# Windowed attention and a gated MLP on one core: two blocks' values with V stationary and sums by ones, first queries scaled in their cast, a negated maximum, and a new order

## The chip, the cores and the metric

The kernel runs on one core of one Trainium2 chip. The metric is device time in microseconds of one execution, as the median over runs; a profile is of one execution. Engines in the tables: PE is TensorE (PEld its weight loads), DVE is VectorE, ACT is ScalarE, POOL is GpSimd, SP is SyncE, which here only issues transfers.

## The reference, cut to what matters

Attention for 4 batches of 8 heads, 768 positions and 64 dimensions a head, in which each position sees the 4 first keys ("sinks") and a window of the 128 last ones; then the heads side by side (512 columns) through two matrices with a quick GELU between.

```python
scores = scale * np.matmul(q, k.transpose(0, 1, 3, 2))        # scale = 1/8
keep = is_sink | in_window                                    # 4 sinks, window 128
scores = np.where(keep, scores, -1000000000.0)
a = np.exp(scores - np.max(scores, axis=-1, keepdims=True))
a = a / (np.sum(a, axis=-1, keepdims=True) + 1e-09)
attn_out = np.matmul(a, v)
x = attn_out.transpose(0, 2, 1, 3).reshape(3072, 512)
h = x @ w_in                                                  # 512 x 2048
g = h * (1.0 / (1.0 + np.exp(-1.702 * h)))
out = g @ w_out                                               # 2048 x 512
```

## The kernel before

**Blocks.** The 3072 positions are 24 blocks of 128; block b is part b % 6 of batch b // 6. They are worked in the order 0, 6, 12, 18 (the first block of each batch, which sees only itself), then 1 to 5, 7 to 11 and so on, which also see the block ahead of them and the sinks. Operations carry the block's number, and "_0" or "_1" for a half, that is four heads.

**A block's operations** and their names: q, k, v are loads with a cast to 16 bits on POOL's queue; tq and tk are its turns on PE (lines 379 to 399 for the first six blocks, of whose loads each partition holds eight neighbouring positions), cq and ck their copies or casts from PSUM into qkT; msk writes the mask of a first block into PSUM ahead of its scores (line 464); sc are the scores (478, 483); mx the row maximum (545); nb the maximum times -1/8 as the bias of the exponential (557), for first blocks alone; bx their exponentials, four instructions a half (568); in the other blocks pk puts the two blocks' scores in one place by a mask (535), sb subtracts the maximum (582) and ex is the exponential (606); ta are turns of the weights on PE (650) and ca their copies into "at"; for later blocks a transfer does that (tat), and sp and so on POOL select what belongs to the own block and to the one ahead (637). ks and vsb prepare the sinks' keys and values, snk are the sinks' scores and ms their maximum.

**Values.** av (line 703) multiplies the turned weights, as the stationary operand, with v65, that is V with a column of ones, 65 columns a head: PSUM gets 128 positions by 4 heads by 65, with the sum of the weights in the last column. nm takes the reciprocal of the four sums (722) and multiplies (723) into xn. tx turns xn back on PE (740), and cx copies it to xT, for the first eight blocks; later ones by a transfer (txd).

**MLP.** Blocks go in groups: [0], [6], [12, 18], then in twos. hG_u is a piece of the first product of group G (786: sixteen matmuls for a single block, four chunks of w_in at a time; wi0 to wi3 are w_in's quarters, and h0_u and h1_u use quarter u). The gate of the first three groups is a tanh on ACT (th, 800) and a product on DVE (g, 807); of the others one activation (816). oB_n is a quarter of the second product of block B (836, quarter n of w_out, loads wo0 to wo3); ev copies it from PSUM and st stores it. The last block's output goes in two pieces, of 320 columns (o23_0 to o23_3) and of 192 (o23_10 to o23_13).

**Buffers** are rings: "mm" in PSUM has three, "sc" two, "av" one. A buffer of "av" holds values or the sinks' scores from the PE step until nm or ms has read it; both kinds take turns in it.

**Order.** The operations are numbered as the program adds them, and ORDER lists all of them in one line of numbers, with a letter where an operation may run on several engines (d for DVE, a ACT, p POOL, s SP). Each engine works off its own in that order, in order. Waits follow from the data and the buffers.

```python
LD, LW, QKX, ATX, XTX, STX, SPX2 = 0.97, 2.55, 1.55, 1.56, 0.77, 0.85, 1.9
NB = {0: (0, 1), 6: (0, 1), 12: (0, 1), 18: (0, 1)}
RING = dict(qkn=4, qkn2=3, e32=3, a16=4, at=4, atp=3, ss=3, xn=3, xt=4, gt1=2, gt2=2, osb=4, mm=3, sc=2, av=1, th=2)
```

Of the kernel before, what the change touches and what calls it, by code (L numbers as in the profile page):

```python
# [54 lines left out]
ORDER = """
1a 9 6 8d 100 15 4a 5a 11 14 7 96 0a 23 94 21 3s 98 17 2s 29 18 104 107 105a 101p 102 103d 16 108 171 20 109 150 19
172a 10 95d 125 110 24 112 225 111 99d 26 151a 113 126d 27 114 115 97d 88 127 106 128a 130 92 226d 116a 117 12 90 129
148 118a 119 13 131 149a 22 120 194 132 121 86 196 195a 135 173 197a 87 133 122 134 89 123 199 124a 200 138 30 136 613
139d 137 25 152 142 174a 140 143 153 614 141d 615 154 91 144 155 619 156 145 157 158 146 616 93 620 147d 159 160 621
637 32 617 634 638 618 176 639 635 631 36 175 636 177 632 610 178 633 161 611 181 35 628 162a 179 612 180 163 182 165  # L60
622 164d 166 629 184 183 33 167 623 185d 168 39 198 630 169 31 204 640 170a 205 188 227 189 641 228a 201 28 230 186
206 642 231 209 202 624 187a 203 215 190 38 643 208 191 207 229 216d 210 644a 192 217 235 211 43 193a 625 232 212a 236
41 280 282 626a 256 281d 258 213 283a 627 233 652 259a 214 237 257a 649 653 218 238 234 261 661 241 40 650 262 654 239
285 37 260 651 662 242 286 304 44 655 266 243a 263 34 219 656 646 663 42 657 658 647 244 220 664 648 659 245 267 670
45 665 660 240 221 671 264 268 246 672 247a 269 265 248 667 222 270 249 666 250 284 668 271 251 48 676 669 46 290 252
323 673 47 253 287 677 291 254 306 272 678 288 255a 674a 223 292 679 273 224a 293 289 682 680d 294 51 307 305 683 50
688 295 308 311 49 686 309 675 52 684 687 312 689 692 310 685 313 276 693 690 314 277 296 315 704 297 344 324 345 705
327 691 316 53 330 325 694 326 361 331 274 695 696 275 328 698 697 681 332 278 317 699 279a 333 329 298 334 318 343
299 700 346 54 347 300 706 55 349 335 701 57 301 350 302 645 319 303a 707 348 702a 352 351 716 708a 320 353 362 336
321 717 354 720 322 337 365 724 709 59 721 363 399 714 364 368 60 712 715 703 369 725 722 366 713 340 355 723 710 341  # L70
367 718 711 356 371 370 338 719 732 64 339 372 726 342 56 733 62 382 381 373 61 383 727 387 384 359 734 360 385 728
388 401 735 390 386 729 374 419 389 750 402 391 375 730d 400 736d 751 748 392 67 406 403 742 66 404 752 65 743 407 749
740 63 753 378 738 379 408 376 739 744 377 393 409 357 405 745 746 358 741 394 420 380 747 439 58 410 754 440 423 421
760 422 426 397 755 427 411 398 761 424 457 756 425 762 428 757 429 430 412 766 758d 438 759 413 767 763 431 444 69
441 770 737 442 71 768 771 445 72 764a 772 769 446 68 416 443 773 780 432 447 417 788 781 433 448 414 774 415 73 458
459 789 775 460 449 464 395 778 396 461 776 418 779 465 782 777 462 436 495 450 783 463 466 790 75 765 437 731 784 467
74 468 434 451 785 435 476 791 482 786d 800 792a 479 454 793 801 798 469 455 794 514 452 795 802 453 808 803 456 477
804 809 478 470 799 483 796 480 471 806 797 485 805 484 816 76 481 810 77 486 474 80 496 475 817 70 502 807 499 487
497 82 811 498 78 500 818 503 81 516 822 504 819 823 505 517 501 812 820a 506 515 821 824 488 518 813 489 825 507 828
814d 83 472 826 552 473 79 519 832 827 521 829 535 836 833 536 522 492 837 834 508 523 830 524 493 509 520 844 831 84  # L80
835 490 534 525 491 845 540 494 541 838 537 846 526 542 839 538 512 787 847 513 543 840 539 544 553 852 848a 545 527
573 864 853 574 590 528 510 841 511 865 559 860 842d 529 546 861 556 862 530 850 547 554 854 851 555 85 560 531 855
856 532 557 858 533 857 561 866 859 558 550 815 562 591 563 551 872 597 867 863 592 564 873 593 598 868 843 594 548
849 880 595 869 596 881 600 565 888 599 549 874 889 870d 566 601 886 875 884 876a 602 567 885 572 568 878 877 575 569
879 892 570 578 882 571 893 603 576 887 890 579 604 894 891 577 883 900 580 581 895 582 901 607 912 608 583 896 913
605 871 897 606 902 898a 910 584 916 911 585 914 917 918 915 908 919 906 909 586 907 903 587 922 588 920 589 923 609
921 904a 928 924 929 925 930 926d 946 931 947 934 942 935 932a 948 943 933 940 905 927 936 941 899 938 937 949 944 939
956 945 950 957 951 958 952 962 953 963 954a 959 964 955 960d 965 961 966d 967
# [67 lines left out]
def kernel(  # L156
# [72 lines left out]
    z_s = plan.add("zs", DVE, 0.25, lambda: nc.vector.memset(vsa, 1.0), key=-897)  # L229
    z_a = [  # L230
# [133 lines left out]
    for pos, b in enumerate(BLOCKS):  # L364
# [5 lines left out]
        qkb = qkT[:, SLOT[b]]  # L370


        buf, n, unit = tunit[b]
        if b in OCT:
            parts = []
            before = used_slot.pop(SLOT[b], [])
            for w in (1, 0):
                tp = ps("mm", (P, 8, 4, 16), FP32, f"t{'qk'[w]}{b}")

                def t_qk(w=w, buf=buf, n=n, tp=tp):  # L380
                    for t in range(8):
                        for l in range(2):
                            nc.tensor.matmul(
                                tp()[64 * l : 64 * l + 64, t], buf()[:, n, w, t],
                                ident.rearrange("p (j l u) -> p l j u", l=2, u=16)[:, l], start=True, stop=True,
                            )
# [5 lines left out]
                parts.append(  # L392
                    plan.add(
                        f"c{'qk'[w]}{b}", {DVE: 0.6, ACT: 0.5}, 0,
                        lambda e, w=w, tp=tp, qkb=qkb: copy(
                            e, qkb[:, 4 * w : 4 * w + 4].rearrange("p c (u t) -> p c u t", t=8),
                            tp().rearrange("p t c u -> p c u t"),
                        ),
                        deps=[a] + before, give=[tp], key=K0 - 40,
                    )  # L400
                )
            o_qkt[b] = parts
        elif b in TQ:
# [37 lines left out]
        if r == 0:  # L441

            def sink_keys(bb=bb, qkb=qkb):
                for hl in range(2):
                    rows = slice(64 * hl, 64 * hl + 64)
                    nc.vector.tensor_copy(
# [3 lines left out]
            o_ks[bb] = plan.add(f"ks{b}", DVE, 0.45, sink_keys, deps=o_qkt[b] + [z_k], key=K0 - 10)  # L450
# [79 lines left out]
        for hf in range(2):  # L530
# [12 lines left out]
            def rowmax(hf=hf, t=sc[hf], own=own, small=small, ms=ms):  # L543
# [156 lines left out]
        for hf in range(2):  # L700
# [34 lines left out]
        if b in TX:  # L735
# [163 lines left out]
```

## Time and profile before

| what | value |
|---|---|
| median of 3 runs (lowest to highest) | 233.0 us (232.78 to 233.21) |
| the profiled execution's own time; its span | 232.43 us; 230.7 us |
| busy: PE, DVE, ACT, POOL | 217.0, 154.5, 139.8, 111.2 us |
| PE's granted clock | 1.00 throughout |
| costliest on PE: first product (L786), second (L836) | 93.2 us in 832, 92.1 us in 400 |
| costliest on DVE: maximum (L545) | 32.7 us in 48 |
| chain that ended last, by engine | PE 35%, ACT 2%, issue 1% |

How to read it: a line of the timeline gives start, time and what ran, with the idle time before it and what ended that in brackets; neighbours on PE overlap, since a matmul's time includes its way through the array, so the pace is read from start to start. A line of groups gives busy time and mean ns of one, then idle time before. A line of stretches gives for each engine its busy time, with the number of instructions in brackets, then PE's clock, the DMA share and GB/s. "DMA to landing" is the time from a transfer's issue to its arrival.

### The profile page before, as it was taken

The numbers are of one execution on the slowest core, as the hardware profiler recorded it, in microseconds if no ns is written. First come the engines' busy times: TensorE is split into PE (matmuls) and PEld (weight loads), VectorE is DVE, ScalarE is ACT, GpSimd is POOL, SyncE is SP. The second block draws the span as 40 slices with busy tenths as digits, with TensorE's granted clock in tenths as the row PEclk, the third lists the DMA queues.
The fourth block names the chain that finished last, engine by engine and source line by source line (L and its number), as shares of the span: only waits on it lengthen the run. The fifth ranks groups of instructions, "written<-read, shape, count | busy, mean of one in ns | idle before, by whom it ended". The sixth has DMA issues, their size and how long they took to land. (4 is left out here: it accounts for less than half of the span.)

```text
span 230.7 us, 5431 instructions
## 1 busy us (share of the span) xinstructions
PE 217.0 (94%) x2202; PEld 151.6 (66%) x2202; DVE 154.5 (67%) x388; ACT 139.8 (61%) x220; POOL 111.2 (48%) x129
## 2 busy tenths in 40 slices
PE   0878899999999999999999999999999999999994
PEld 0666865876586686486577496486686686775863
DVE  2487899999979976987797848668577847121001
ACT  2278774874597687168378386786358486631531
POOL 8983435995393869077392619265350312300000
PEclk9999999999999999999999999999999999999999
DMA  5999999999999899999999989999647542402312
GB/s 76 167 189 200 206 198 180 168 134 91 153 182 168 159 242 131 148 162 135 165 196 136 196 172 131 131 185 110 140 92 114 142 99 45 99 0 45 114 71 91
DMA packets 120904, 32.07 MB, mean 139 GB/s; under 512 B 112016, under 2 KB 117936, under 8 KB 120880
## 3 DMA queue, kind: packets, MB, share of 16 engines
q0 software_dynamic: 69888, 13.64, 72.2%
q1 hardware_dynamic: 50512, 17.96, 38.7%
q8 instruction: 17, 0.28, 0.5%
q10 hardware_dynamic: 480, 0.13, 0.3%
q14 instruction: 7, 0.06, 0.1%
HBM read 27.46 MB, written 6.29 MB: 146 GB/s over the span
## 5 line engine op out<-in xcount | busy, mean ns | idle before, releaser
L786 PE MATMUL hT<-xT,w_in 128*128 128x256 f16 (+1 forms) x832 | 93.2, 264 | 1.5 <-ACT gT L816 0.5
L836 PE MATMUL o<-w_out,gT 128*128 128x512 f16 (+2 forms) x400 | 92.1, 371 | 0.0
L786 PEld LDWEIGHTS <-w_in 128*128 128x128 f16 x832 | 73.9, 98 | 14.1 <-issue 3.7
L816 ACT ACTIVATE gT<-hT 128x512 f16<-128x512 f32 x80 | 45.8, 597 | 33.1 <-PE hT L786 32.9
L836 PEld LDWEIGHTS <-gT 128*128 128x128 f16 x400 | 36.1, 98 | 33.3 <-issue 1.9
L637 POOL TENSOR_SCALAR_AFFINE_SELECT atp<-at 128x1024 f16<-128x1024 f16 (+1 forms) x22 | 22.3, 1015 | 72.9 <-DMA at<-a 69.9
L545 DVE TENSOR_REDUCE mx<-sc 128x4 f32<-128x512 f32 x48 | 32.7, 683 | 0.8 <-PE sc L478 0.5
L606 ACT ACTIVATE a<-e 128x1056 f16<-128x1056 f32 (+2 forms) x24 | 22.5, 938 | 15.4 <-issue 12.5
L535 DVE COPY_PREDICATED sc<-later,sc 128x512 f32<-128x512 uint16 x40 | 26.8, 689 | 3.6 <-PE sc L483 3.3
L582 DVE TENSOR_TENSOR e<-sc,mx 128x512 f32<-128x512 f32 x40 | 26.7, 684 | 0.7
L722 DVE RECIPROCAL rcp<-av 128x4 f32<-128x4 f32 x48 | 8.6, 179 | 24.0 <-PE av L712 22.1
L637 POOL TENSOR_SCALAR_AFFINE_SELECT at<-at 128x1024 f16<-128x1024 f16 (+1 forms) x22 | 22.2, 1009 | 1.4
L271 POOL DMA_DIRECT2D v<-in_v_dram x24 | 21.7, 906 | 2.0 <-DMA w_in<-in_moe_w_in_dram 1.2
L723 DVE TENSOR_TENSOR xn<-av,rcp 128x256 f16<-128x256 f32 x48 | 20.4, 424 | 1.7
L241 DVE COPY osb<-o 128x512 f32<-128x512 f32 (+2 forms) x10 | 6.3, 634 | 21.2 <-PE o L836 21.1
L606 ACT ACT_TABLE_LOAD x12 | 15.4, 1283 | 6.1 <-DVE e L596 4.0
L318 POOL DMA_DIRECT2D qkn<-in_q_dram x18 | 16.1, 897 | 4.5 <-DMA w_out<-in_moe_w_out_dram 1.6
L816 ACT ACT_TABLE_LOAD x13 | 16.7, 1283 | 2.4 <-PE hT L786 1.8
L318 POOL DMA_DIRECT2D qkn<-in_k_dram x18 | 16.0, 890 | 3.6 <-DMA w_out<-in_moe_w_out_dram 3.4
L710 PE MATMUL av<-v,at 128*128 128x65 f16 x192 | 17.5, 195 | 0.1
L710 PEld LDWEIGHTS <-at 128*128 128x128 f16 x192 | 14.4, 98 | 2.7 <-DVE at L241 0.3
L712 PE MATMUL av<-v,atp 128*128 128x65 f16 x160 | 15.1, 194 | 0.0
(58 smaller groups left out, 198.1 us busy)
## 6 DMA issues: line engine op xcount, KB each, us to landing
out_dram<-osb SPq DMA_DIRECT2D x23, 256.0 KB, 3.2
qkn<-in_q_dram POOLq DMA_DIRECT2D x24, 128.0 KB, 5.7
qkn<-in_k_dram POOLq DMA_DIRECT2D x24, 128.0 KB, 5.4
v<-in_v_dram POOLq DMA_DIRECT2D x24, 128.0 KB, 5.5
w_in<-in_moe_w_in_dram POOLq DMA_DIRECT2D x4, 512.0 KB, 10.4
w_out<-in_moe_w_out_dram POOLq DMA_DIRECT2D x4, 512.0 KB, 15.4
at<-a SPq DMA_TRANSPOSE x18, 3.7
qkT<-qkn SPq DMA_TRANSPOSE x10, 4.3
```

Of the source, the lines that this page charges most:

```text
L271: f"v{b}", POOL, 0.88, lambda b=b, view=view: nc.gpsimd.dma_start(v65[:, b, :, 0:D], view),
L318: lambda buf=buf, n=n, w=w, view=view: nc.gpsimd.dma_start(buf()[:, n, "qk".index(w)], view),
L535: nc.vector.copy_predicated(out=t()[:, :, :, own].rearrange("p l j s -> p (l j) s"), mask=later.unsqueeze(1).to_broadcast((P, 4, P)), data ...
L545: nc.vector.tensor_reduce(out=part, in_=t()[:, :, :, own], axis=AX.X, op=ALU.max)
L582: nc.vector.tensor_tensor(out=e32()[:, 512 * hf : 512 * hf + 512].rearrange("p (l j s) -> p l j s", l=2, j=2), in0=t()[:, :, :, own], in1= ...
L606: nc.scalar.activation(out=a16()[:, lo:hi], in_=e32()[:, lo:hi], func=AF.Exp, scale=scale)
L637: nc.gpsimd.affine_select(out=dst, in_=at()[:, lo : lo + num], pattern=[[0, num], [1 if own else -1, P]], compare_op=ALU.is_ge if own else ...
L710: nc.tensor.matmul(av()[:, i], at()[:, c], v65[:, b, h], start=(r == 0), stop=(r == 0))
L723: nc.vector.tensor_tensor(out=xn()[:, xi, 4 * hf : 4 * hf + 4].rearrange("p (j l) d -> p l j d", l=2), in0=av()[:, :, 0:D].rearrange("p (l ...
L786: nc.tensor.matmul(ht()[:, n].rearrange("p (n t) -> p n t", n=NT), w_in16[:, c, bass.ts(f, P)], t0()[:, i0 : i0 + NT, c], start=(c == 0), ...
L816: lambda fs=fs, gt=gt, ht=ht: nc.scalar.activation(out=gt()[:, fs[0] : fs[-1] + 1], in_=ht(), func=AF.Gelu_apprx_sigmoid),
L836: nc.tensor.matmul(po()[:, 0:width], gt()[:, F, bass.ts(t, P)], w_out16[:, F, c0 : c0 + width], start=(F == 0), stop=(F == NF - 1),)
```

## The change

1. **Values of blocks 0 and 6** (AVT). V is stationary, 64 columns a head, and the turned weights stream. Two heads' outputs lie one under the other, on partitions 0 to 63 and 64 to 127, as 64 dimensions by 128 positions: already the form of xT. The sums come from a product of a 128 x 64 matrix of ones with the weights, so each of the 64 partitions holds the sum of its column. A half of a block takes two matmuls of 256 columns and four of 128 where it took four of 65. The normalization takes the reciprocal of 256 numbers a partition and multiplies 256, straight into xT. tx0, tx6, cx0 and cx6 go; one memset of the ones (zo) comes.
2. **First blocks' queries** (NEGATE, blocks 0, 6, 12, 18) get the factor 1/8 in their cast; the row maximum is written negated and is itself the bias; the eight nb go.
3. **The sinks' keys** may be copied on POOL too; here all stay on DVE. Some costs in the plan's table are other numbers; they have no effect on what is emitted.
4. **A new ORDER.**

```diff
+NEGATE = True
+AVT = {0,6}
 ...
+    ones = const.tile([P, D], FP16, name="ones")
+    z_o = plan.add("zo", DVE, 0.12, lambda: nc.vector.memset(ones, 1.0), key=-890)
 ...
+        prescaled = NEGATE and b in NB
+        qf = [scale if prescaled else 1.0, 1.0]
 ...
                         lambda e, w=w, tp=tp, qkb=qkb, qf=qf: copy(
                             e, qkb[:, 4 * w : 4 * w + 4].rearrange("p c (u t) -> p c u t", t=8),
-                            tp().rearrange("p t c u -> p c u t"),
+                            tp().rearrange("p t c u -> p c u t"), qf[w],
                         ),
 ...
+                if neg:
+                    nc.vector.tensor_reduce(out=part, in_=t()[:, :, :, own], axis=AX.X, op=ALU.max, negate=True)
+                    return
 ...
-                    nbias = const.tile([P, 8], FP32, name=f"nb{b}")
+                    nbias = small if prescaled else const.tile([P, 8], FP32, name=f"nb{b}")
 ...
-                o = plan.add(f"nb{b}_{hf}", DVE, 0.09, neg, deps=[o], key=K0 - 29)
-                def bexp(hf=hf, t=sc[hf], own=own, a16=a16, nbias=nbias):
+                if not prescaled:
+                    o = plan.add(f"nb{b}_{hf}", DVE, 0.09, neg, deps=[o], key=K0 - 29)
+                def bexp(hf=hf, t=sc[hf], own=own, a16=a16, nbias=nbias, scale=1.0 if prescaled else scale):
 ...
+        for hf in range(2 if b in AVT else 0):
+            av = ps(AVR.get((b, hf), "av"), (P, 2, 2, P), FP32, f"av{b}_{hf}")
+            rc = sb("e32", (P, 2, P), FP32, f"rc{b}_{hf}")
+            xt, ti = xts[b]
+            def turned(hf=hf, av=av, at=at, b=b):
+                for l in range(2):
+                    rows = slice(64 * l, 64 * l + 64)
+                    c = 4 * hf + 2 * l
+                    nc.tensor.matmul(av()[rows, 1], ones, at()[:, c : c + 2], start=True, stop=True)
+                for l in range(2):
+                    rows = slice(64 * l, 64 * l + 64)
+                    for jj in range(2):
+                        c = 4 * hf + 2 * l + jj
+                        nc.tensor.matmul(
+                            av()[rows, 0, jj], v65[:, b, head(c), 0:D], at()[:, c], start=True, stop=True
+                        )
 ...
+            def norm_t(hf=hf, av=av, rc=rc, xt=xt, ti=ti):
+                nc.vector.reciprocal(out=rc(), in_=av()[:, 1])
+                nc.vector.tensor_tensor(out=xt()[:, ti, 2 * hf : 2 * hf + 2], in0=av()[:, 0], in1=rc(), op=ALU.mult)
 ...
-        for hf in range(2):
+        for hf in range(0 if b in AVT else 2):
 ...
-        if b in TX:
+        if b in AVT:
+            pass
+        elif b in TX:
```

**The order's beginning**, by engine, with the numbers read back into names. Before:

```
PE   tq0 msk0 tk0 sc0 tk18 tq12 tk6 tk2 ta0_0 tq6 msk6 ta0_1 tk12 av0_0 sc6 tk1 av0_1 tq1 tq18 tx0 snk1 ta6_0
     h0_1 av6_0 ta6_1 msk12 sc12 av6_1 h0_3 tx6 h0_2 h1_3 h1_2 msk18 h1_1 sc18 h0_0 ta12_0 h1_0 ta12_1 av12_0
     o0_0 ta18_0 av12_1 o0_1 sc1 tx12 o6_0 av18_0 tq2 o6_1 snk2
DVE  zs zk zv za1 z1 ck0 mx0_0 za0 vsb0 nb0_0 mx0_1 vsb2 nb0_1 ck6 vsb1 ks0 ck2 za2 ks6 za3 nm0_0 mx6_0 mx6_1
     nb6_0 nm0_1 ms1 nb6_1 ca6_0 ks12 nm6_0 ca6_1 g0_1 mx12_0 nb12_0 nm6_1 mx12_1 cx6
ACT  ident own identb bias0 cq0 ck18 bx0_0 cq12 bx0_1 cq6 ca0_0 ca0_1 ck12 ck1 cq1 bx6_0 cx0 bx6_1 cq18 th0_1
POOL q0 k0 k18 q12 k6 k2 q6 vsb3 v0 k12 v6 q18 k1 q1 wi1 wi3 wi2 v12 wi0 wo0 wo1 q2 v18 wo2 wo3 k3 q4 k4 q3
SP   vsa3 vsa1 vsa0 later vsa2 bias1
```

After:

```
PE   msk0 tq0 tk0 tk6 sc0 tq6 tk18 ta0_0 tk12 tq1 msk6 ta0_1 sc6 tq18 tk1 av0_0 tq12 ta6_1 av0_1 msk12 ta6_0 sc12
     snk1 h0_1 av6_0 ta12_0 tk2 av6_1 msk18 ta12_1 sc18 av12_0 tq2 h0_0 h1_0 h1_1 av12_1 h0_2 tx12 sc1 ta18_0
     h1_3 h1_2 snk2 h0_3 o0_0 o6_0 av18_0 o0_1 sc2 o6_1
DVE  zv zs za2 za1 z1 za0 vsb1 cq0 ck6 mx0_0 zk mx0_1 ck18 ks0 vsb2 ks6 ck12 zo za3 mx6_1 mx6_0 cq18 nm0_0 ks18
     nm0_1 ks12 mx12_0 ms1 mx12_1 nm6_0 nm6_1 g0_1 mx18_1 mx18_0 cq2 nm12_0 g0_0 g1_0 nm12_1 g1_1 g0_2 pk1_0
ACT  bias1 own ident later ck0 cq6 bx0_0 bx0_1 ca0_0 cq1 ca0_1 bx6_1 bx6_0 ck1 cq12 ca6_0 ca6_1 bx12_0 bx12_1
POOL q0 k0 k6 q6 k18 k12 q1 k1 q18 v0 q12 wi1 v6 k2 v12 vsb0 q2 vsb3 wi0 wi2 wi3 wo0 wo1 v18 wo2 wo3 q3 k3 k4
SP   identb bias0 vsa1 vsa2 vsa3 vsa0
```

At the end PE's last operations were ... o23_11 o23_3 o23_12 o23_13 and are ... o23_12 o23_2 o23_13 o23_3.

More of the change, by code (lines that the diff above doesn't have):

```diff
@@ L41 @@
 LH = 1.0
+OCTDT = "FP32"
 HW = set()
@@ L45 @@
 AHEAD = 4
+AVT = set()
+NEGATE = False
 TQ = set(BLOCKS[:8])
@@ L85 @@
[L85 to L88, printed above, removed]
+2a 8d 5s 16 0s 4a 9 13 1a 12 97 15 7 11 3a 99 18 19 101 108 24 95 21 28 98d 105 27 103 106d 25 104a 122 17 109 123d
@@ new lines @@
+124 22 110 125a 162 89 6 112 111 163d 20 113 107d 114 30 141 100d 185 115a 23 126d 127 186a 142d 116 96p 128 10 14
+117a 164 131 183 31 129 118 132 102p 165d 143 130 119 135 87 166d 120 184a 91 146 144a 121 93 133 147 145d 134a 188 88
+148 602 136a 189 90 149 150 137 26 151 138 152 214 92 139 153a 94 167 603 140 154 215a 168 604 155a 156 171 216 34 599
+169 172 217d 617 600 157 620 618 601 33 170 158 619 605 159 621 160 606 187 622 161a 607 36 173 626 190 174a 193 623
+627 191 219 608 37 628 624 220 611 625 609 194 629 195 29 177 612 192 39 610 218 196 630 199 221 197 224 175 178 176a
@@ new lines @@
+631 225 200 179 613 201a 180 226 202 181 632 222 40 229 614 182d 633a 203 223 198 235 38 227 650 615a 236a 43 245 247
+651 246d 641 32 248d 228 652 250 269 642 44 271 251 249 272d 270a 204 643 237 230 274 231 205a 252 644 293 232a 206
+255 635 42 275 645 256 634 638 233 636 616 646 41 208 637 639 656 207 209 653 640 234 257 45 659 654 253 657 238 239
+655 660 50 658 647 254 46 665 240 648 48 258 259 210 649 273 47 211 661 260 276 49 279 241 35 666 242 280 662 312 277
+295 212 663a 667 281 213a 243 282 278 668 244a 296 283 679 669a 261 294 680 673 284 300 262 297 671 298 675 51 672 664
@@ new lines @@
+301 674 670 677 52 299 676 681 53 303 302 678 314 313 682 315 693 304 319 316 265 683 317 285 694 320 305 286 685 266
+318 350 263 54 686 321 695 264 55 332 322 289 56 335 684 687 323 290 306 267 338 333 688 334 307 336 287 696 268a 324
+288 59 339 689 697a 57 337 308 291 340 58 690 292a 341 309 342 713 691a 310 343 707 714 311 705 692 388 352 351 708
+353 699 354 325 355 709 700 698 357 326 703 710 358 706 711 62 704 359 327 61 712 356 701 328 60 370 702 360 329 361
+344 715 330 376 721 331 345 373 371 716 372 362 65 374 722 64 377 390 717 63 375 723 378 379 718 391 380 346 719a 381
@@ new lines @@
+724 347 727 725d 408 729 363 728 735 364 389 736 733 720 392 382 730 395 365 737 393 66 366 743 67 738 394 734 367 68
+396 731 383 397 749 732 368 409 71 398 399 348 70 750 349 412 741 369 410 744 742 411 400 413 386 745 415 446 387 739
+416 751 740 414 746 418 417 401 384 419 747d 752 385 748 69 765 753d 402 757 766 420 428 427 74 767 430 754 72 433 755
+768 73 429 758 434 763 484 756 431 403 764 761 436 421 435 777 432 759 404 422 405 760 447 75 406 762 771 453 437 76
+407 450 448 778 77 449 454 769 451 438 772 770 452 425 779 455 456 773 426 457 465 780 471 783 458 781a 439 486 789
@@ new lines @@
+520 848 841 579 521 843 838 535 842 543 839 832 544 844 546 853 536 840 549 518 845 547 551 550 855 846 519 854 849
+552 522 539 580 540 861 586 850 583 553 581 856 582 584 862 587 851 589 537 588 852 863 554 585 867 538 590 555 864
+857 865d 868 591 561 873 567 564 556 874 875 557 568 869 876 592 565 558 870 877 559 593 570 871 569 560 878 566 889
+872 866 571 881 596 858 597 890 882 594 891 595 859a 895 860 879 572 896 903 880 907 904 905 908 573 892 899 893a 574
+883 900 906 897 901 898 884 902 577 909 578 911 910 575 912 576 917 598 913 885 914 918 915d 886 929 887d 919 888 916
@@ L89 @@
+923 920 924 930 933 927 934 921a 925 922 935 894 926 928 937 936 931 938 939 932 945 940 951 946 941 952 942 953 943a
+947 954 944 948 955d 956 949a 950
 """
@@ L377 @@
             for w in (1, 0):
-                tp = ps("mm", (P, 8, 4, 16), FP32, f"t{'qk'[w]}{b}")
+                tp = ps("mm", (P, 8, 4, 16), FP16 if OCTDT == "FP16" else FP32, f"t{'qk'[w]}{b}")
                 def t_qk(w=w, buf=buf, n=n, tp=tp):
@@ L393 @@
                     plan.add(
-                        f"c{'qk'[w]}{b}", {DVE: 0.6, ACT: 0.5}, 0,
-                        lambda e, w=w, tp=tp, qkb=qkb: copy(
+                        f"c{'qk'[w]}{b}", {DVE: 0.65 if OCTDT == "FP32" else 0.38, ACT: 0.5}, 0,
+                        lambda e, w=w, tp=tp, qkb=qkb, qf=qf: copy(
                             e, qkb[:, 4 * w : 4 * w + 4].rearrange("p c (u t) -> p c u t", t=8),
-                            tp().rearrange("p t c u -> p c u t"),
+                            tp().rearrange("p t c u -> p c u t"), qf[w],
                         ),
@@ L420 @@
                         f"c{'qk'[w]}{b}", {DVE: 0.36, ACT: 0.49}, 0,
-                        lambda e, w=w, tp=tp, qkb=qkb: copy(e, qkb[:, 4 * w : 4 * w + 4], tp()[:, 4 * w : 4 * w + 4]),
+                        lambda e, w=w, tp=tp, qkb=qkb, qf=qf: copy(
+                            e, qkb[:, 4 * w : 4 * w + 4], tp()[:, 4 * w : 4 * w + 4], qf[w]
+                        ),
                         deps=[a] + before, give=[tp], key=K0 - 40,
@@ L441, with sink_keys @@
         if r == 0:
-            def sink_keys(bb=bb, qkb=qkb):
+            def sink_keys(e, bb=bb, qkb=qkb):
                 for hl in range(2):
                     rows = slice(64 * hl, 64 * hl + 64)
-                    nc.vector.tensor_copy(
+                    (nc.vector if e == DVE else nc.gpsimd).tensor_copy(
                         out=ksb[rows, bb, :, 4 * hl : 4 * hl + 4], in_=qkb[rows, 4:8, 0:4]
                     )
-            o_ks[bb] = plan.add(f"ks{b}", DVE, 0.45, sink_keys, deps=o_qkt[b] + [z_k], key=K0 - 10)
+            o_ks[bb] = plan.add(f"ks{b}", {DVE: 0.45, POOL: 0.6}, 0, sink_keys, deps=o_qkt[b] + [z_k], key=K0 - 10)
         e32 = sb("e32", (P, 8 * P + 32), FP32, f"e32_{b}")
@@ L699 @@
         norms = []
-        for hf in range(2):
+        for hf in range(2 if b in AVT else 0):
[14 more added lines that the diff above has]
+                        )
+            o = plan.add(
+                f"av{b}_{hf}", PE, 0.5 if early else 0.44, turned, deps=[ld["v", b], o_at[hf], z_o],
+                take=[av], give=[at], key=K0 - 22,
+            )
+            def norm_t(hf=hf, av=av, rc=rc, xt=xt, ti=ti):
+                nc.vector.reciprocal(out=rc(), in_=av()[:, 1])
+                nc.vector.tensor_tensor(out=xt()[:, ti, 2 * hf : 2 * hf + 2], in0=av()[:, 0], in1=rc(), op=ALU.mult)
+            norms.append(
+                plan.add(f"nm{b}_{hf}", DVE, 0.75, norm_t, deps=[o], take=[xt, rc], give=[av, rc], key=K0 - 32)
+            )
+            norms[-1].deps += norms[:-1]
+            o_x[b] = norms[-1]
+        for hf in range(0 if b in AVT else 2):
             av = ps(AVR.get((b, hf), "av"), (P, 4, D1), FP32, f"av{b}_{hf}")
```

36 lines of the change are left out of this document (6 added, 30 removed).

## The prediction

> **What bounds the kernel now.** I read the page first, then stretches of the span, the timelines of the start, and the loads' landings.
>
> ```profile
> span 230.7 us, 5431 instructions
> ...
> core 0: us, PE busy (x) PEld busy (x) DVE busy (x) ACT busy (x) POOL busy (x), PEclk, DMA share, GB/s
> 5.00:25.00 20.00, 15.62 (x300) 12.37 (x301) 13.78 (x40) 12.04 (x33) 14.41 (x20) 1.00 1.38 188
> 25.00:40.00 15.00, 14.82 (x195) 10.58 (x193) 13.28 (x35) 9.68 (x25) 6.40 (x8) 1.00 1.50 194
> 40.00:60.00 20.00, 19.85 (x207) 14.01 (x206) 19.23 (x47) 12.68 (x26) 15.15 (x20) 1.00 1.84 134
> 60.00:100.00 40.00, 39.66 (x377) 27.14 (x376) 33.36 (x85) 28.02 (x37) 23.50 (x25) 1.00 1.55 172
> ```
>
> PE is full from about 25 us on (14.82 of 15, 19.85 of 20, 39.66 of 40). So the end is set by when PE gets through its opening work, then a fixed amount of PE work, then the tail. Of PE's idleness that a change could take away, 4.4 us lie between 5 and 25. VectorE is nearly full from 40 to 60 (19.23 of 20), so lateness that it brings there is not made up.
>
> The opening also depends on loads, which land one behind the other. The rows are the issues of the first and the last quarter of w_in and of block 18's values, each with its landing.
>
> ```profile
> L324 POOL DMA_DIRECT2D w_in<-in_moe_w_in_dram x1: 891/891/891, 10.9 to 10.9; - x1
> DMA to landing us min/median/max: 7.7/7.7/7.7
> ...
> L324 POOL DMA_DIRECT2D w_in<-in_moe_w_in_dram x1: 847/847/847, 14.1 to 14.1; - x1
> DMA to landing us min/median/max: 13.0/13.0/13.0
> ...
> L271 POOL DMA_DIRECT2D v<-in_v_dram x1: 907/907/907, 18.9 to 18.9; - x1
> DMA to landing us min/median/max: 15.6/15.6/15.6
> ```
>
> They land at 18.6, 27.1 and 34.5. Between the first two there are three weight quarters and v12: 2.5 us a quarter and 1.0 for a block's 128 KB. v18 has the same loads ahead of it in the new order, so it lands at 34.5 in both. The four quarters of w_in have one load more ahead of them (q2), so the last lands at 28.1; counted back from there by the new POOL order, wi2 lands at 25.6, wi0 23.1, q2 20.6, v12 19.6, k2 18.6, v6 17.6, wi1 16.6, v0 13.1. After them wo0 lands at 30.6 and wo1 at 33.1.
>
> **What goes.** The old kernel's start, PE first, then ScalarE, then VectorE:
>
> ```profile
> 5.68 0.64 PE L383 MATMUL tq<-ident,qkn 128*64 128x64 f16 x16 [5.68 <-DMA qkn<-in_q_dram]
> ...
> 12.70 0.58 PE L650 MATMUL ta<-ident,a 128*128 128x128 f16 x4 [1.24 <-ACT qkT L245]
> 13.21 0.64 PE L383 MATMUL tq<-ident,qkn 128*64 128x64 f16 x16
> 13.78 1.03 PE L464 MATMUL sc<-bias,identb 128*128 128x256 bf16 x4
> 14.61 0.63 PE L650 MATMUL ta<-ident,a 128*128 128x128 f16 x4
> 15.74 0.40 PE L710 MATMUL av<-v,at 128*128 128x65 f16 x4
> ...
> 11.03 1.14 ACT L568 ACTIVATE a<-sc,nb 128x128 f16<-128x128 f32 x4 [0.26 <-DVE nb L557]
> ...
> 16.18 0.18 DVE L722 RECIPROCAL rcp<-av 128x4 f32<-128x4 f32 x1 [0.90 <-PE av L710]
> 16.40 0.42 DVE L723 TENSOR_TENSOR xn<-av,rcp 128x256 f16<-128x256 f32 x1
> L557 DVE TENSOR_SCALAR nb<-mx x8: 151/162/359, 10.6 to 31.5; 128x4 f32<-128x4 f32 x8
> ```
>
> Eight nb instructions of 0.16 us (one took 0.36) lie between a maximum and its exponentials. With the scale in the cast and the maximum written negated they go, and cost nothing elsewhere: the cast and the reduction are there anyway. The first mask moves ahead of the first queries, into PE's 5.68 us of waiting, since identb and bias0 are now first on SP. I walk the new order with these durations: tq0 at 5.9 (ident is now third on ScalarE's queue, so 0.2 later), sc0 at 7.9 behind tk6, the first exponentials at 9.6 against 11.03, ta0_0 at 10.7 against 12.70. PE runs at the slow pace of these rows (0.5 to 0.6 for a group, 0.83 for a mask), so ta0_0, tk12, tq1, msk6, ta0_1, sc6, tq18 and tk1 take 5.0 and av0_0 starts at 15.7, against 15.74. The two us go into work that is brought forward; the first values come no sooner.
>
> **What PE does instead.** Warm rows:
>
> ```profile
> 34.41 0.40 PE L740 MATMUL tx<-ident,xn 128*128 128x128 f16 x4
> 34.64 1.03 PE L836 MATMUL o<-w_out,gT 128*128 128x512 f16 x4
> 35.51 0.29 PE L710 MATMUL av<-v,at 128*128 128x65 f16 x4
> 35.72 0.44 PE L383 MATMUL tq<-ident,qkn 128*64 128x64 f16 x16
> 48.65 2.79 PE L786 MATMUL hT<-xT,w_in 128*128 128x256 f16 x24
> 51.28 1.04 PE L836 MATMUL o<-w_out,gT 128*128 128x512 f16 x4
> ```
>
> From start to start: four transposes of x 0.23, four values 0.21, a matmul of 256 columns 0.11 (2.63 by 24), of 128 columns half of that. A new values step (two of 256, four of 128) is 0.44 one after the other and 0.22 if the two column halves overlap fully: 0 to 0.23 more for each of four, against 0.46 saved by two turns of x. That is -0.46 to +0.46, in a time when PE waits for VectorE or loads; I take nothing. The two casts of x that go (one on each engine) took 0.42 on VectorE and 0.6 on ScalarE and stood in the way of h0 and h1; the new chain below is without them.
>
> **What VectorE does instead.** This term decides. Nothing in the trace divides more than four numbers a lane:
>
> ```profile
> L722 DVE RECIPROCAL rcp<-av x48: 166/182/184, 16.2 to 206.8; 128x4 f32<-128x4 f32 x48
> L520 DVE COPY ss<-snk x16: 175/191/193, 37.9 to 178.5; 128x32 f32<-128x32 f32 x16
> L241 DVE COPY osb<-o 128x320 f32<-128x320 f32 x1 | 0.5, 493 | 14.3 <-PE o L836 14.3
> L241 DVE COPY osb<-o 128x192 f32<-128x192 f32 x1 | 0.4, 358 | 0.1
> ```
>
> Copies from PSUM cost 1.05 ns an element (493 less 358, over 128) on some 0.158 us, so four elements would take 0.162; the copy of 32 fits (0.191). The reciprocal of four takes 0.182. The 20 ns over can be a fixed price of the operation or 5 ns an element. For 256 elements the first gives 0.45 us, the second 0.16 + 256 x 6.05 ns = 1.71. The excess comes with the one operation that divides, so I put it down to the elements and take 1.71. The 20 ns are good to about 6, hence 1.3 to 2.1; 0.45 stays as the other end.
>
> The Trainium skill ("VectorE: DVE Perf Modes", First, the fixed hardware budget) calls the reciprocal an iterated divide with a repeat count of 8. Read as eight cycles an element at its 0.96 GHz, an estimate would be 0.16 + 256 x 8.33 ns = 2.29 us and the sum some 2.3 us higher; four elements would take 0.19 by it, near the row's 0.182.
>
> A normalization then takes 1.71 + 0.04 + 0.42 = 2.17 us where it took 0.64 (16.18 to 16.82). All four stand in one chain: "av" has a single buffer that only the normalization gives back, and the sinks' scores take it too. The walk, with 0.6 from start to start for a mask, maximum, cast or gate on VectorE, and 0.87 for an h or o unit on PE:
>
> | step | reciprocal 1.71 | reciprocal 0.45 |
> |---|---|---|
> | av0_0; nm0_0 (behind cq18) | 15.7; 16.2 to 18.3 | 15.7; 16.2 to 17.1 |
> | av0_1; nm0_1 (behind ks18) | 18.3; 18.7 to 20.8 | 17.2; 17.6 to 18.4 |
> | snk1, then h0_1 | 20.9 | 18.8 |
> | av6_0 (behind ms1); nm6_0 (behind mx12_1) | 22.0; 22.6 to 24.7 | 19.7; 20.2 to 21.0 |
> | av6_1; nm6_1 | 24.7; 25.0 to 27.1 | 21.3; 21.7 to 22.5 |
> | av12_0, tq2, h0_0, h1_0, h1_1 end | 30.2 | 26.2 |
> | tx12 (behind nm12_1, after g0_0 and g1_0) | 31.9 | 27.3 |
> | sc1, ta18_0, h1_3, h1_2, snk2, h0_3, o0_0, o6_0 end | 37.3 | 33.1 |
> | av18_0 | 37.3 | 34.5 (waits for v18) |
>
> The old kernel starts av18_0 at 35.51. By then the new order has not done o0_1 (0.87) but has done tq2 and snk2 (0.38 and about 0.1): it owes 0.4 more. With the slow reciprocal that is 37.3 - 35.5 + 0.4 = 2.2 us.
>
> **The tail.**
>
> ```profile
> 227.60 0.82 SPq L856 DMA_DIRECT2D out_dram<-osb  x2
> out_dram<-osb SPq DMA_DIRECT2D x1, 96.0 KB, 1.7
> ```
>
> The last piece is now the one of 320 columns: an eviction longer by 0.14 (493 less 358), and a store of 160 KB, which has 1.7 us for 96 KB as its lower bound: about +0.2 in all.
>
> **Sum**: 2.2 + 0.2 = 2.4. The profiled execution took 232.43 us around its span of 230.7, so 234.8 on its scale; the median of the runs shown, 233.0, lies 0.57 above it, so 235.4 there, which I round to 235.5.
>
> **Rivals.** *The reciprocal is as quick as a copy* (0.45). Then VectorE hides it, and PE reaches av18_0 when v18 lands: 34.5 - 35.5 + 0.4 + 0.2 = -0.4, so 232.6, on the other side. For it: the 20 ns may be a fixed price. The point from which it fails is a reciprocal of about 0.9, where four normalizations eat the 1.4 us for which PE waits for v18.
>
> *Eight cycles an element*: four times 0.58 more, 237.8. Against it: the four-element row lies 8 ns below what it asks.
>
> *The later order stalls.* Counted in PE work, block 23 has 15.3 us between its scores and its first values where it had 18.7 in the old order. Against it: block 5 had 15.9, and it lies in the stretch from 60 to 100 that keeps PE busy for 39.66 of 40. One us of stall with a quick reciprocal gives 233.6.
>
> **How the numbers follow.** Slow reciprocal 0.62, eight cycles 0.06, quick 0.27, later stall 0.05. The likeliest gives 235.5, its own range 234.0 to 237.0 from a reciprocal of 1.3 to 2.1 (0.4 either way, four times). The whole range reaches down to the quick one: 232.4 to 237.0. About 0.2% (0.5 us) is what a measurement of this kernel can tell from no change. The quick case, at -0.4 and good to 0.6, splits into 0.15 faster and 0.11 same; with a little from the others, faster is 0.16, same 0.12 and slower 0.72.
>
> **What would show it.** The row of the new reciprocal, 128x256: a mean of 1.3 to 2.1 us, or near 0.45. h0_1 starts near 20.9, or 18.8; av18_0 near 37.3, or 34.5. No nb rows; first exponentials near 9.6. With the slow reciprocal PE's idle time between 5 and 40 us grows by some 2 us, and past 60 it is as before. The forecast is wrong if the reciprocal is quick, or if it is slow and PE finds other work meanwhile, so that av18_0 still starts before 35.5.

## The result, and the profile after

The changed kernel takes 242.0 us (240.39 to 243.04), the old one 233.11 on the same chip: a ratio of 1.0376, interval 1.0339 to 1.0413. The forecast was 235.5 with a range to 237.0. The profiled execution is the slowest of six, 243.04 us around a span of 241.3. The kernels' times are medians of all runs; without the slow runs those of the copy and of the three copies are 233.27 and 239.85.

The group of the new reciprocal, on VectorE (busy time, mean ns of one, idle time before):

```profile
L740 DVE RECIPROCAL rc<-av 128x256 f32<-128x256 f32 x4 | 7.0, 1755 | 1.4 <-PE av L730 1.4
```

1.755 us against the 1.71 that the forecast took. VectorE's timeline shows the four:

```profile
16.95 1.75 DVE L740 RECIPROCAL rc<-av 128x256 f32<-128x256 f32 x1
...
19.75 1.76 DVE L740 RECIPROCAL rc<-av 128x256 f32<-128x256 f32 x1
...
24.64 1.76 DVE L740 RECIPROCAL rc<-av 128x256 f32<-128x256 f32 x1 [0.66 <-PE av L730]
...
27.60 1.76 DVE L740 RECIPROCAL rc<-av 128x256 f32<-128x256 f32 x1 [0.74 <-PE av L730]
```

PE's timeline beside it; the bracket gives PE's wait and what ended it:

```profile
6.53 0.64 PE L392 MATMUL tq<-ident,qkn 128*64 128x64 f16 x16 [2.12 <-DMA qkn<-in_q_dram]
...
19.21 0.30 PE L725 MATMUL av<-at,ones 128*64 128x256 f16 x2 [1.62 <-DVE xT L741]
...
22.03 0.27 PE L518 MATMUL snk<-ksb,qkT 128*128 128x8 f16 x4 [1.31 <-DVE xT L741]
22.16 1.87 PE L836 MATMUL hT<-xT,w_in 128*128 128x128 f16 x16
...
26.91 0.43 PE L725 MATMUL av<-at,ones 128*64 128x256 f16 x2 [1.22 <-DVE xT L741]
...
30.78 4.58 PE L836 MATMUL hT<-xT,w_in 128*128 128x128 f16 x48
...
42.32 0.29 PE L758 MATMUL av<-v,at 128*128 128x65 f16 x4
```

The waits for the single av buffer are the ones that the walk had. But look at the first products: 48 matmuls of 128 columns take 4.58, where the walk has 0.87 for sixteen. Block 18's values start at 42.32, not at 37.3. The granted clock (the number behind the five engines) says why. The rows are stretches of 3.4 us, with PE's busy time first:

```profile
17.36:20.78 3.42, 1.73 (x25) 1.13 (x23) 3.34 (x5) 2.01 (x6) 3.42 (x5) 1.00 1.42 175
20.78:24.19 3.41, 2.16 (x24) 1.94 (x26) 3.06 (x8) 1.93 (x7) 2.03 (x3) 0.50 1.24 205
24.19:27.60 3.41, 2.19 (x33) 1.49 (x30) 2.18 (x2) 2.54 (x7) 0.87 (x1) 0.50 1.24 203
27.60:31.02 3.42, 3.03 (x39) 2.17 (x39) 3.38 (x5) 0.58 (x1) 0.96 (x2) 0.50 1.23 197
31.02:34.43 3.41, 3.41 (x35) 3.41 (x33) 2.39 (x5) 1.74 (x5) 1.17 (x2) 0.50 1.53 193
```

After a stretch with PE busy for 1.73 of 3.42 us the clock is halved, and it stays so from 20.8 to 34.4 us. It comes back after a stretch that is full. Longer stretches of this kernel, the first three as the prediction has them for the old one:

```profile
5.00:25.00 20.00, 14.48 (x250) 11.22 (x250) 14.96 (x31) 11.03 (x33) 16.45 (x22) 0.89 1.42 185
25.00:40.00 15.00, 13.26 (x190) 11.61 (x189) 12.15 (x21) 8.73 (x21) 4.37 (x5) 0.69 1.47 193
60.00:100.00 40.00, 39.63 (x392) 27.08 (x391) 34.89 (x87) 28.12 (x38) 29.13 (x32) 1.00 1.61 161
150.00:200.00 50.00, 47.92 (x442) 32.27 (x439) 36.63 (x92) 32.32 (x41) 18.13 (x18) 1.00 0.90 110
```

The old kernel from 150 to 200:

```profile
150.00:200.00 50.00, 50.00 (x462) 34.92 (x460) 32.47 (x82) 33.43 (x43) 17.97 (x18) 1.00 0.68 118
```

From 25 to 40 PE is busy for 13.26 of 15 us, which looks little worse than 14.82; at a clock of 0.69 it does much less in that time. Busy time alone hides the loss. From 150 to 200 PE is idle for 2.1 us that the old kernel does not have.

### The profile page after: what moved, and what is told of

The parts are those of the page before. It is cut to its first block, busy times and chain, and to the rows that moved or that the text cites. A ratio compares the mean times of both kernels' runs of the same rounds, so it can differ in the third digit from the quotient of the medians.

```text
span 241.3 us, 5434 instructions
## 1 busy us (share of the span) xinstructions
PE 223.4 (93%) x2202; PEld 155.3 (64%) x2202; DVE 160.1 (66%) x378; ACT 142.4 (59%) x222; POOL 112.2 (46%) x130
## 4 chain that ended last, share of the span: by engine, by line
PE 63%; DVE 16%; DMA 11%; ACT 4%; POOL 3%; issue 2%; POOLq 0%; SPq 0%; DVEq 0%; ACTq 0%
PE hT L836 29%; PE o L886 23%; DMA at<-a 6%; DVE rc L740 3%; DMA xT<-xn 3%; PE sc L494 2%; DMA qkn<-in_k_dram 2%; DVE mx L559 2%; DVE mx L562 2%; PE av L758 2%; DVE e L597 2%; DVE sc L546 2%; PE av L760 1%; PE av L753 1%; DVE gT L857 1%
## 5 line engine op out<-in xcount | busy, mean ns | idle before, releaser
L836 PE MATMUL hT<-xT,w_in 128*128 128x256 f16 (+1 forms) x832 | 95.6, 270 | 1.5 <-DMA xT<-xn 1.5
L886 PE MATMUL o<-w_out,gT 128*128 128x512 f16 (+2 forms) x400 | 93.1, 371 | 0.0
L836 PEld LDWEIGHTS <-w_in 128*128 128x128 f16 x832 | 76.7, 101 | 16.1 <-issue 3.5
L546 DVE COPY_PREDICATED sc<-later,sc 128x512 f32<-128x512 uint16 x40 | 26.2, 690 | 11.2 <-PE sc L494 11.0
L559 DVE TENSOR_REDUCE mx<-sc 128x4 f32<-128x512 f32 x40 | 27.3, 682 | 0.1
L770 DVE RECIPROCAL rcp<-av 128x4 f32<-128x4 f32 x44 | 7.8, 177 | 22.5 <-PE av L760 22.4
L248 DVE COPY osb<-o 128x512 f32<-128x512 f32 (+1 forms) x9 | 5.8, 653 | 21.3 <-PE o L886 21.3
L771 DVE TENSOR_TENSOR xn<-av,rcp 128x256 f16<-128x256 f32 x44 | 18.7, 424 | 1.5
L758 PE MATMUL av<-v,at 128*128 128x65 f16 x176 | 16.4, 195 | 1.4 <-POOL at L652 1.0
L758 PEld LDWEIGHTS <-at 128*128 128x128 f16 x176 | 13.5, 98 | 4.5 <-POOL at L652 1.6
```

What stands on the lines that cost most here:

```text
L546: nc.vector.copy_predicated(out=t()[:, :, :, own].rearrange("p l j s -> p (l j) s"), mask=later.unsqueeze(1).to_broadcast((P, 4, P)), data ...
L758: nc.tensor.matmul(av()[:, i], at()[:, c], v65[:, b, h], start=(r == 0), stop=(r == 0))
L771: nc.vector.tensor_tensor(out=xn()[:, xi, 4 * hf : 4 * hf + 4].rearrange("p (j l) d -> p l j d", l=2), in0=av()[:, :, 0:D].rearrange("p (l ...
L836: nc.tensor.matmul(ht()[:, n].rearrange("p (n t) -> p n t", n=NT), w_in16[:, c, bass.ts(f, P)], t0()[:, i0 : i0 + NT, c], start=(c == 0), ...
L886: nc.tensor.matmul(po()[:, 0:width], gt()[:, F, bass.ts(t, P)], w_out16[:, F, c0 : c0 + width], start=(F == 0), stop=(F == NF - 1),)
```

## The experiments

**The reciprocal as a copy.**

```diff
-                nc.vector.reciprocal(out=rc(), in_=av()[:, 1])
+                nc.vector.tensor_copy(out=rc(), in_=av()[:, 1])
```

> The changed kernel with one difference: the reciprocal of the 256 sums is a copy of the same shape, so blocks 0 and 6 are multiplied by their sums and not divided. Theory (the four reciprocals of 1.755 us make PE wait, and the waits let its clock fall to half from 21 to 34 us; that is all of the loss): the copy takes 0.42 us, the granted clock stays at 1.00, values of block 18 start near 34.5 us, the time is 232.6, within 231.8 and 233.8. Rival (the new order is slow by itself, in its loads or in its later part): 236 or more, with the late waits for transfers of x still there.

Measured: 233.48 us, ratio 0.9998 (0.9966 to 1.003), granted clock 0.999. Lines of its groups, of VectorE's and PE's timelines and of its stretches:

```profile
L740 DVE COPY rc<-av 128x256 f32<-128x256 f32 x4 | 1.7, 418 | 0.8 <-PE av L730 0.8
...
16.37 0.41 DVE L740 COPY rc<-av 128x256 f32<-128x256 f32 x1
...
23.82 2.85 PE L836 MATMUL hT<-xT,w_in 128*128 128x128 f16 x48
...
34.13 0.30 PE L758 MATMUL av<-v,at 128*128 128x65 f16 x4 [0.25 <-DMA v<-in_v_dram]
...
150.00:200.00 50.00, 47.84 (x451) 33.93 (x449) 34.71 (x80) 34.29 (x43) 15.25 (x16) 1.00 0.60 97
```

The 48 first products take 2.85, and block 18's values wait for their load and start at 34.13, as the quick column of the walk had it (34.5); but the wait is 0.25 us, where the walk had 1.4 (33.1 to 34.5). So the whole loss, 8.5 us, hangs on the reciprocals. The rest of the change is worth nothing that shows: the opening is 1.4 us ahead of the old kernel's 35.51, but from 150 to 200 us PE is busy for 47.84 of 50.

**The old values in the new order.** The set of blocks with V stationary is empty; tx0 and cx0 stand ahead of snk1, tx6 and cx6 behind nm6_1, the copies on VectorE.

```diff
-AVT = {0,6}
+AVT = set()
```

> The new order with the old values step: 65 columns, reciprocal of four, turn of x on PE and its copy on VectorE for blocks 0 and 6; the rest of the change stays. Theory: 232.3 to 234, clock 1.00, since nothing wide is divided. Rival (the order is slow by itself): 236 or more.

Measured: 234.83 us, ratio 1.0044 (1.0012 to 1.0076), clock 0.998. The new order by itself is not the loss; with the old values step it is about 1 us slower than the old order, outside the expected band by 0.8.

**The scaled queries and the negated maximum alone.** As the last, but in the old order, from which the eight nb are taken.

> The old kernel in its old order with the scaled first queries and the negated maximum alone: the eight nb go, nothing else moves. Theory (PE reaches its work when the loads land, so a shorter start is worth little): 232.4 to 233.3, first exponentials 0.3 to 1 us earlier. Rival (the first chain sets the end): 231.5 to 232.3.

Measured: 233.6 us, ratio 1.0002 (0.9974 to 1.0029). Lines of ScalarE's and PE's timelines:

```profile
10.47 1.15 ACT L583 ACTIVATE a<-sc,mx 128x128 f16<-128x128 f32 x4
...
34.86 0.29 PE L758 MATMUL av<-v,at 128*128 128x65 f16 x4
```

The first exponentials come 0.56 us earlier (11.03 before) and block 18's values 0.65 earlier (35.51 before); the time does not move: 0.3 above the expected band, beside an old kernel that takes 233.3 here. The rival, that the first chain sets the end, falls.

**PE's waits filled.** Matmuls that stand there anyway are issued again into the same place:

```diff
+FILL = {"tq12": 5, "msk12": 4, "h0_1": 2, "tk2": 5, "msk18": 2}
 ...
-                    for t in range(8):
+                    for t in list(range(8)) * again:
```

> The changed kernel, reciprocals as they are, with PE's waits between 17 and 29 us filled by repeats of matmuls that stand there anyway (tq12 five times, msk12 four times, h0_1 twice, tk2 five times, msk18 twice; ta6_0 is moved ahead of msk12). The results are the same. Theory (about half of the loss is the fallen clock): granted clock 1.00, one first-product unit 0.87 us in place of 1.53, values of block 18 near 38.5 us in place of 42.3, the time 237 to 239. Rival (VectorE's chain sets the pace and the slow clock costs nothing): the clock stays at 1.00 too, but the time is within 1 us of the changed kernel's 242.

> As the kernel with PE's waits filled, but h0_1 once and tk2 four times, so that values of block 6 are not held up by the filling. Theory (the filling itself cost 0.5 us before values of block 6, and the rest of what it did not win was lost between 60 and 100 us by where things fell): clock 1.00, block 18's values near 39.3, time 239.5 to 240.5. Rival (the fallen clock costs only the 1.2 us that the first filling won): 240.8 or more, although block 18's values start before 40.

The first filling takes 240.77 us (ratio 1.0309, 1.0255 to 1.0364), the lesser one 237.55 (1.0192, 1.0139 to 1.0245); the clock is at 1.00 in both. Lines of the lesser one's timelines (VectorE, then PE) and stretches, then of the first one's:

```profile
15.96 1.75 DVE L741 RECIPROCAL rc<-av 128x256 f32<-128x256 f32 x1
...
28.15 0.30 PE L759 MATMUL av<-v,at 128*128 128x65 f16 x4 [0.79 <-DVE xT L742]
...
28.75 2.85 PE L837 MATMUL hT<-xT,w_in 128*128 128x128 f16 x48
...
38.71 0.28 PE L759 MATMUL av<-v,at 128*128 128x65 f16 x4
...
17.49:20.90 3.41, 2.67 (x34) 2.19 (x34) 3.27 (x7) 1.62 (x4) 2.67 (x5) 1.00 1.29 199
24.31:27.73 3.42, 2.43 (x58) 1.85 (x50) 2.83 (x4) 2.21 (x5) 1.00 (x2) 1.00 1.24 209
```

```profile
16.78 1.75 DVE L741 RECIPROCAL rc<-av 128x256 f32<-128x256 f32 x1
...
39.89 0.29 PE L759 MATMUL av<-v,at 128*128 128x65 f16 x4
...
60.00:100.00 40.00, 38.30 (x373) 25.78 (x372) 33.69 (x83) 27.71 (x37) 24.99 (x27) 1.00 1.70 157
```

Both miss their bands, the first by 1.8 us above, the lesser by 2.0 below; each rival, that the slow clock costs nothing or only 1.2 us, falls too, the first narrowly. With more work on PE the kernel is faster: by 1.2 us with the first filling, where the intervals of the ratios overlap with the changed kernel's, and by 4.4 with the lesser one, where they do not. In both, ta6_0 also stands one place earlier; that move was not run alone.

The two starts differ by 0.8 us (first reciprocals at 15.96 and 16.78), so block 18's values have to be counted from the first reciprocal. From there they come after 25.37 us in the changed kernel (16.95 to 42.32), 23.11 in the first filling and 22.75 in the lesser one: the fallen clock costs 2.3 us at this place by the first filling and 2.6 by the lesser one. The 3.2 us between the two fillings at the end lie mostly behind it. The first one loses again between 60 and 100 us, where PE is busy for 38.30 of 40 against the changed kernel's 39.63; why its later part fell out worse was not settled. What is left with the clock up, 237.55 less 233.48 of the copy, is 4.1 us: the wait for VectorE itself.

**Three and five copies in place of the reciprocal.**

```diff
-                nc.vector.reciprocal(out=rc(), in_=av()[:, 1])
+                for _ in range(3):
+                    nc.vector.tensor_copy(out=rc(), in_=av()[:, 1])
```

> The changed kernel with each reciprocal replaced by three copies of the same shape one after the other, some 1.1 us (blocks 0 and 6 are multiplied by their sums). Theory (what counts is only how long VectorE holds the single av buffer; with the one copy PE waited 0.25 us for block 18's values, so there is next to no slack): four times 0.68 more than one copy, 2.7 us, so 236.2 with the granted clock at 1.00, or 238 if the clock falls here too. Rival (a normalization of up to 0.9 to 1.1 us is hidden behind the loads, as the prediction had it): within 1 us of the one copy's 233.5.

> The same with five copies, some 1.8 us, as long as the reciprocal takes (1.755), and no reciprocal of 256 anywhere. Theory (duration alone): the same time as the changed kernel, 241 to 243, granted clock 0.97. Rival (something else in the reciprocal, such as a port or a drain, costs too): less than 240.

Three take 1.33 us (not 1.1) and the kernel 240.21 us (ratio 1.0346, 1.0261 to 1.0431; the medians alone, 240.21 over 233.32, give 1.0295; clock 0.993). Five take 2.25, and the kernel 243.59 (1.0451, 1.0402 to 1.0501; clock 0.972). Lines of VectorE, of PE and stretches, of the three, then of the five:

```profile
16.71 1.33 DVE L741 COPY rc<-av 128x256 f32<-128x256 f32 x3
...
37.88 0.29 PE L759 MATMUL av<-v,at 128*128 128x65 f16 x4
...
15.69:19.10 3.41, 1.55 (x42) 1.26 (x37) 3.14 (x9) 3.10 (x10) 3.40 (x6) 1.00 1.60 188
19.10:22.52 3.42, 3.29 (x35) 2.68 (x34) 3.21 (x10) 1.57 (x4) 2.19 (x4) 0.50 1.25 211
22.52:25.93 3.41, 2.22 (x43) 1.70 (x41) 2.63 (x6) 3.20 (x10) 1.56 (x2) 1.00 1.23 202
```

```profile
16.60 2.25 DVE L741 COPY rc<-av 128x256 f32<-128x256 f32 x5
...
43.47 0.29 PE L759 MATMUL av<-v,at 128*128 128x65 f16 x4
...
14.43:17.84 3.41, 1.80 (x66) 1.50 (x64) 2.98 (x6) 2.90 (x10) 3.39 (x5) 1.00 1.72 178
17.84:21.25 3.41, 1.51 (x22) 1.09 (x22) 3.07 (x10) 1.51 (x4) 3.41 (x6) 1.00 1.37 187
```

With 0.42, 1.33, 1.755 and 2.25 us in this place the kernel takes 233.5, 240.2, 242.0 and 243.6; the five lie 0.6 above their band. The reciprocal lies in the row of the copies, so its duration alone counts and nothing peculiar to the operation shows. The opening tells how much of it is hidden. The table counts from the start of the first copy or reciprocal to block 18's values, beside the one copy's 17.76 us plus four times what the step takes over 0.42:

| kernel | step | measured | reckoned | stretches at half clock |
|---|---|---|---|---|
| one copy | 0.42 | 17.76 | 17.76 | 0 |
| three copies | 1.33 | 21.17 | 21.4 | 1 |
| lesser filling | 1.755 | 22.75 | 23.1 | 0 |
| first filling | 1.755 | 23.11 | 23.1 | 0 |
| the change | 1.755 | 25.37 | 23.1 | 4 |
| five copies | 2.25 | 26.87 | 25.1 | 4 |

Next to nothing of a longer step is hidden there, and four stretches at half clock cost about 2 us on top. The end of the kernel follows less neatly: the three copies are 3.7 us behind the one copy at block 18's values (37.88 and 34.13), but 6.7 in the medians, more than the theory's 238 allows. What the later part adds was not settled.

**The price of the reciprocal.** To the old kernel are added, on VectorE near the end where it is idle, reciprocals and copies of several sizes.

> The old kernel with a memset, and with reciprocals and copies of 4, 32, 64, 128, 256 and 512 numbers a partition added on VectorE near the end, where it is idle; the outputs stay. Price by the element: reciprocal 0.16 us and 6.2 ns an element, so 0.36, 0.56, 0.95, 1.75 and 3.3 us from 32 to 512; a fixed price instead would have shown 1.755 only for what is peculiar to the changed kernel (PSUM as source). Copies of the same about 1 ns an element or less, as the source here is SBUF.

Groups, mean ns behind the busy time:

```profile
L868 DVE RECIPROCAL sizes<-sizes 128x512 f32<-128x512 f32 x1 | 3.4, 3353 | 0.0
L868 DVE RECIPROCAL sizes<-sizes 128x256 f32<-128x256 f32 x1 | 1.8, 1754 | 0.0
L868 DVE RECIPROCAL sizes<-sizes 128x128 f32<-128x128 f32 x1 | 1.0, 953 | 0.0
...
L868 DVE RECIPROCAL sizes<-sizes 128x64 f32<-128x64 f32 x1 | 0.6, 553 | 0.0
...
L868 DVE RECIPROCAL sizes<-sizes 128x4 f32<-128x4 f32 x1 | 0.2, 178 | 0.0
```

3353 less 1754 over 256 elements is 6.25 ns an element, the same between 128 and 64, on 0.153 us. The one run takes 232.43 us, within the 232.15 to 234.4 of the old kernel beside it, so the idle stretch seems to have taken them all.

**One block, and the old order.** The first keeps V stationary for block 0 alone (AVT = {0}, tx6 and cx6 put back); the second puts the new values step alone into the old order (NEGATE = False, without tx0, cx0, tx6 and cx6).

> The changed kernel with V stationary for block 0 alone; block 6 has the old values, the reciprocal of four, its turn of x on PE (right behind the second normalization) and its copy on VectorE. Two of the four wide reciprocals stay. Theory (each wide reciprocal holds the single av buffer for 1.3 us more than a copy, and the clock falls only when such waits follow one another): granted clock 1.00 or one step of 3.4 us at half, 2.7 us more than the quick kernel's 233.5, so 236 to 237.5. Rival (the first waits alone bring the clock down as far as in the changed kernel): 0.97 to 0.98 and 238.5 to 241.

> The old kernel in its old order with V stationary for blocks 0 and 6 alone (tx0, cx0, tx6, cx6 go, the ones are set late on VectorE); queries, nb and the loads as before. Theory (the reciprocal's duration is the loss, whichever the order): 4 to 9 us above the old kernel, 237 to 242, with the same waits of PE for the av buffer. Rival (the old order, which puts first-product units between the values of block 6, hides the four reciprocals): within 2 us of 233.3.

One block: 237.08 us, ratio 1.013 (1.0074 to 1.0186), clock 0.984. Old order: 239.12 us, 1.0223 (1.0174 to 1.0271), clock 0.978. Stretches of the first, then PE's timeline and a stretch of the second:

```profile
16.32:19.73 3.41, 1.53 (x23) 1.17 (x18) 3.17 (x6) 2.17 (x7) 3.35 (x6) 0.99 1.53 192
19.73:23.14 3.41, 2.44 (x31) 2.07 (x29) 3.27 (x8) 1.84 (x6) 2.16 (x3) 0.50 1.24 208
23.14:26.56 3.42, 3.10 (x39) 2.43 (x38) 1.73 (x6) 2.93 (x9) 1.06 (x2) 0.51 1.24 205
```

```profile
18.57 0.30 PE L725 MATMUL av<-at,ones 128*64 128x256 f16 x2 [1.30 <-DVE xT L741]
...
21.96 0.25 PE L518 MATMUL snk<-ksb,qkT 128*128 128x8 f16 x4 [2.48 <-DVE xT L741]
...
17.16:20.57 3.41, 1.02 (x42) 0.83 (x38) 3.38 (x6) 1.89 (x5) 0.91 (x1) 1.00 1.24 206
```

Two wide reciprocals are enough to bring the clock down, for two stretches; the time is within the theory's band, the clock between the two expectations. In the old order the same waits stand ahead of the second values and of the sinks' scores, and the clock falls there too. But in one of its four runs the mean clock reads 0.999, and its 238.98 us are no better than the 238.93 to 239.59 of the other three. No trace of that run is kept, and the column also reads 1.00 before the clock's first rise (see the last section), so it cannot tell a clock that stayed up from one that rose late. What a fallen clock costs at the end of a kernel therefore stays open; shown is what it costs at block 18's values. No version here beats the old kernel: the best are its equals.

## Why the prediction was wrong

*The reciprocal's price* was right. 5 ns an element over a copy's, read from 20 ns on four elements, gave 1.71 us; it is 1.755, or 5.2 ns an element over the copy's 0.418. At 6.25 ns an element neither the 8.33 of the eight cycles nor the copy's price held.

*The step that failed* is the walk's "0.87 for an h or o unit on PE", together with the steps of its chain; the sum took the loss in the opening as 2.2 us. "av18_0 | 37.3" is 42.32, so 5.0 us were missing, in three parts:

- The pace. With PE waiting for half of a 3.4 us stretch the clock was halved for 13.6 us, and the first products took 1.5 us a unit (4.58 for three; 2.85 with the clock up). The sum had no term for this; the fillings put 2.3 or 2.6 us on it.
- The chain was right in kind: the single av buffer makes each wide reciprocal a wait of PE, first ahead of the second values, then ahead of the sinks' scores. But the walk has 21.1 us from the first reciprocal to block 18's values (16.2 to 37.3), and the fillings took 22.75 and 23.11 with the clock up. A few tenths were missing at each step, 1.7 or 2.0 us in all.
- In the profiled execution the first reciprocal started at 16.95 and not at 16.2, with tq0 at 6.53 and not at 5.9: 0.75 us.

*"PE's idle time between 5 and 40 us grows by some 2 us, and past 60 it is as before"*: it grew from 4.6 to 7.3 us, but work at half pace counts as busy, so this is no measure of the loss. Past 60 it is not as before: 2.1 us came between 150 and 200. By block 18's values the changed kernel is 6.8 us behind (42.32 against 35.51), 7.2 with the 0.4 owed; the profiled executions differ by 10.6 (243.04 less 232.43), the medians by 8.9. The rest comes later, and only these 2.1 us of it are located.

*What goes, and PE's own work*: at nothing, as priced; the 1.6 us at the first transposes (11.12 against 12.70) and the negated maximum are not seen in the time, alone or with the rest.

*The quick rival* had the time right, measured as an experiment: 34.13 for 34.5, and 233.48 for 232.6, whose difference lies in the interval. Its room for a longer reciprocal it had wrong: PE waited 0.25 us for block 18's load and not 1.4, so little could be hidden behind it. Its point of failure, a reciprocal of 0.9 us, was not tried; 1.33 is far beyond it. *The later order* got 0.05 for a stall; the copy's kernel, too, shows about 2 us of PE idle from 150 to 200 where the old one had none, more than the 1.4 that its opening gained. The new order with the old values shows 0.3 there, so the order alone does not fix it.

## What to carry to other kernels

Price a reciprocal by the numbers a lane that it divides: spreading sums over partitions to save a turn makes 256 divisions out of 4. And where PE waits on another engine in an opening, count PE's busy share in stretches of some 3.4 us beside its idle time: here, below about half, the work behind the wait ran at half pace too. Where PE will wait anyway, repeated work of no use can be cheaper than silence (237.55 us against 242.0).

## What the runs showed of the hardware

In the stretches looked at here, the clock fell after PE was busy for 1.73, 1.55, 1.51, 1.53 and 1.02 us of 3.41, and stayed after 1.80, 2.22, 2.43 and 2.67, in the first filling even after 1.72 (169.88 to 173.29). It came back after stretches of 3.41, 3.29 and 3.10, and not after 3.03. The Trainium skill ("TensorE: Matmul & The Clock Gate", What's actually happening) lets the clock fall after an idle window of 3.4 us; the period agrees (20.8 to 34.4 us is four of them), but the stretch was not idle: PE was busy for half of it.

The slow start is not in the clock column, nor in the "1.00 throughout" of the table of before. The column reads 1.00 in these first microseconds, yet the pace there is the slow one. The first record of the clock in the trace is at 17.36 us in the changed kernel and at 14.07 in the lesser filling; that the clock was low until then is read from the pace alone. The rows are the turn of block 18's queries in the changed kernel, and the five turns of block 12's in the lesser filling:

```profile
15.04 0.64 PE L392 MATMUL tq<-ident,qkn 128*64 128x64 f16 x16
```

```profile
14.83 1.40 PE L393 MATMUL tq<-ident,qkn 128*64 128x64 f16 x78
```

16 take 0.64 in the one, 78 take 1.40 in the other at the same time of the span. The first values start at 15.91 and at 14.58; 0.99 us of this lies already between the first turns of the weights (11.12 and 10.13), so the earlier rise is worth some 0.3.
